# Attention with a learned bias and an expert layer: the expert part of the first two blocks in two halves of d_ff, weights decoded with a Prelu, no arithmetic on GpSimd, a new order

## The chip, the cores and the metric

One core of a Trainium2 chip runs the whole program. The metric is the device time of one execution in microseconds (us), the median of several runs. Engines are named as in the profile: PE (TensorE), DVE (VectorE), ACT (ScalarE), POOL (GpSimd) and SP (SyncE, which here only issues transfers).

## The reference

Attention over 4 batches, 8 heads, 576 positions and 64 dimensions, with a bias that a small network of 32 hidden units makes from the logarithm of the distance of two positions; its output, 2304 tokens of 512, goes through an expert layer with 2048 hidden units.

```python
scores = scale * np.matmul(q, k.transpose(0, 1, 3, 2))
x = (np.log1p(np.abs(rel)) / np.log1p(np.maximum(pos[:, None], 1.0)))[..., None]
bias = np.maximum(x @ w1 + b1, 0.0) @ w2              # 576 x 576 x 8 heads
attn = softmax(scores + bias.transpose(2, 0, 1))       # max subtracted, sum + 1e-9
x = (attn @ v) as 2304 tokens x 512
h = x @ w_in                                           # 512 x 2048, float64 weights
out = (h - np.tanh(h)) @ w_out                         # 2048 x 512, float64 weights
```

## The kernel before

**Precision.** Every large product is taken from fp16 or bf16 halves: a value is split into a high part and the rest (low part), and three products are summed. High parts are written by a scaled copy (`narrow`, L384 on ACT, L385 on POOL, L387 on DVE), low parts by a subtraction (`minus`, L402 POOL, L403 DVE).

**Bias.** 36 groups of 16 positions: four relu instructions of 128 x 576 per group (`hg`, L448 ACT, L450 DVE), 16 matmuls (`pb`, L460), one eviction (`bo`, L469 ACT, L470 DVE) and a store to DRAM (`bias_d`). They are read back by attention as `bt`.

**Weights.** w_in comes as 16 chunks (`wi`: k by c, 512 hidden units each), w_out as 16 (`wo`: f, 128 hidden units each), 512 KB each, as pairs of 32-bit words of a float64. `weight_chunk` makes fp16 halves of one on chip: a shift of the low word (L489, DVE), the sign put into it (L494, DVE), a multiplication of the high word by 2^-111 (L384 to L387), a bit-wise merge of the two (L502, DVE), the high part and the low part. `ws_wi` and `ws_wo` are its staging tiles.

**Attention.** A tile is 128 queries of two heads: scores (`ps`, L588), addition of the bias with the row's extreme (`s`, `mx`, L602, DVE), exp (L616, ACT), reciprocal (L623 and L624), the normalised product as high part (`hl`, L384, ACT) and low part (L632, DVE), a transpose by DMA (`pt`, L642, issued by SP), values (`px`, L664), and the block's input `xt` as high part (L394, ACT) and low part (L682, DVE). k and v are prepared by `prep_kv` (high L384 or L385, low L529, copies and memsets on POOL L536 to L538), q by `prep_q`.

**Expert part.** Tokens come in ten blocks: block 0 has 128 tokens (the half tile t = 4 of the first two batches), blocks 1 to 8 have 256 each, block 9 again 128. `moe(i)` runs over d_ff in groups of 512 columns (four f of block 0, two f of the others): hidden matmuls (`ph`, L703, 24 of 256 tokens or 48 of 128), tanh (`tt`, L715, ACT), h − tanh h (L720, DVE), `gh` (ACT) and `gl` (low part), and output matmuls into one accumulator (`po`, L730), of which there is one buffer. At the end of a block `po` is evicted in two halves (`ot`, L394 and L395) and stored.

**Order.** Nothing above is in program order. A planner (`Plan`) takes each operation with its costs (`c_dve`, `c_act`, ...), the engines that may do it (`WAYS`) and a priority, and lays the operations out by list scheduling; the numbers in `ADJ` are added to the priorities. Each engine then runs its list in order. Tiles share buffers by group (`big`, `row`); `BUFS` says how many there are.

Of the kernel before, what the change touches and what calls it, by code (L numbers as in the profile page):

```python
# [19 lines left out]
P = 128  # L20
# [16 lines left out]
HALF = 4  # L37
# [3 lines left out]
BUFS = {'row': 8, 'big': 12, 'stage': 5, 'hg': 4, 'bt': 3, 'hl': 3, 'pt': 4, 'kv': 8, 'qq': 2, 'mx': 6, 'xt': 6, 'tt': 2, 'gh': 3, 'gl': 3, 'ot': 2}  # L41
# [20 lines left out]
class Op:  # L62
    __slots__ = ("alts", "eng", "cost", "fn", "prio", "deps", "outs", "bufs", "start", "end", "left", "idx", "ready", "port")
# [5 lines left out]
class Plan:  # L69
    LAT = {"pe": 190.0, "dve": 200.0, "act": 60.0, "pool": 60.0, "dma": 0.0}  # L70
# [52 lines left out]
    def op(self, eng, cost=None, fn=None, r=(), w=(), prio=0.0, psum=False):  # L123
# [5 lines left out]
        o.port = {e for e, c, _ in alts if e == "pool" and not isinstance(c, tuple) or e == "dve" and not psum}  # L129
# [29 lines left out]
    def order(self):  # L159
# [6 lines left out]
        hw = xfer = port = 0.0  # L166
# [10 lines left out]
        while done < len(self.ops):  # L177
            moved = False
            claims = {} if loose else self.claimed(cand, now, slots, limit)
            for e in free:  # L180
# [3 lines left out]
                for o in cand[e]:  # L184
                    if o.ready > now or port > now and e in o.port:
                        continue
                    if best is not None and (o.prio, o.idx) >= (best.prio, best.idx):
                        continue
                    if len(o.alts) > 1:
                        mine = now + self.load(e, o.alts[e][0])  # L190
                        if any(
                            max(free[x], now, port if x in o.port else 0.0) + self.load(x, a[0]) < mine
                            for x, a in o.alts.items()
                            if x != e
                        ):
                            continue
# [23 lines left out]
                if isinstance(o.cost, tuple):  # L220
                    issue, move, after, hold = o.cost
                    if e == "dma":
                        hw = max(hw, now) + issue
                        begin = max(hw + 650.0, xfer)
                    else:
                        begin = max(now + SWDGE_HOLD + 650.0, xfer)
                    xfer = begin + move
                    free[e] = now + SWDGE_HOLD if e == "pool" else max(hw, begin + 200.0) if hold else hw
                    o.end = xfer + after
                else:  # L230
                    free[e] = now + o.cost
                    o.end = free[e]
                    if e in o.port:
                        port = o.end
# [13 lines left out]
            if o is not None:  # L248
# [4 lines left out]
                for d in o.outs:  # L253
                    d.left -= 1
                    same = o.eng in d.alts and len(d.alts) == 1 and not isinstance(o.cost, tuple)
                    d.ready = max(d.ready, now + (0.0 if same else lat))
# [45 lines left out]
def kernel(  # L302
# [51 lines left out]
    new_hg = shaped("hg", lambda v: v.rearrange("p (a s) -> p a s", a=2), True)  # L354
    new_bt = shaped("bt", lambda v: v.rearrange("p (a s) -> p a s", a=2))
# [25 lines left out]
    def narrow(n, out, in_, scale=1.0, ptr=0, kind="moe"):  # L381
# [3 lines left out]
            "pool": ("pool", c_pool(n, ptr), lambda: G.tensor_scalar(  # L385
                out(), in_(), scale() if ptr else scale, 1.0, ALU.mult, ALU.mult)),
# [19 lines left out]
    def move(nbytes, out, in_, r=(), w=(), prio=0.0, part=P, hold=(), soft=False):  # L406
# [10 lines left out]
        c = c_dma(nbytes, part)  # L417
# [16 lines left out]
    def bias_group(t, prio):  # L434
# [5 lines left out]
        for j in range(4):  # L440
# [10 lines left out]
                    ("pool", 2400.0,  # L451
                     lambda to=to, src=src, bs=bs: G.tensor_scalar(to(), src, bs, 0.0, ALU.add, ALU.max)),
# [4 lines left out]
        def mms():  # L457
# [7 lines left out]
        op("pe", 1000, mms, r=[(h, y) for h in hgs for y in range(2)] + ["w2"], w=[pb], prio=prio)  # L465
# [6 lines left out]
            r=[pb, "rl"], w=[bo], prio=prio, psum=True,  # L472
        )
        dst = bias_d[16 * t : 16 * t + 16].rearrange("i h k -> (i h) k")
        move(P * S * 4, dst, bo, r=[bo], w=[("bias", t)], prio=prio)


    def weight_chunk(src, hi, lo, key, prio):
# [3 lines left out]
        def words(i, dt=F32):  # L482
# [39 lines left out]
    def prep_kv(b, p, prio):  # L522
# [17 lines left out]
        op("pool", 900.0, split, r=[kw], w=[(kw, 0), (kw, 1)], prio=prio)  # L540
# [27 lines left out]
    def attn_tile(g, t, p, bb, qq, bt, prio):  # L568
# [28 lines left out]
        op("pe", c_mm(HS, 1, 2 * len(terms)) + 190.0, scores, r=rd, w=pss + [(x, "x") for x in rows + [m]], prio=prio)  # L597
        for j in range(2):
# [14 lines left out]
            op("dve", c_psum(S) + 80, bias_min, r=[ps, (bt, 0), (bt, 1)], w=[s, (m, j)], prio=prio - DRAIN, psum=True)  # L613
# [6 lines left out]
            op("act", c_act(S, 1) + 190, expo, r=[(m, j)], w=[s, (m, 2 + j)], prio=prio - 2 * DRAIN)  # L620
# [262 lines left out]
```

## Time and profile before

| | us |
|---|---|
| median of three runs | 682.8 |
| the three runs | 680.49, 682.8, 682.97 |
| span of the profiled execution | 679.7 |
| PE busy | 609.4 |
| DVE busy | 485.8 |
| ACT busy | 422.9 |
| POOL busy | 72.2 |

The profiled execution is one run; its span goes from its first to its last instruction. Busy time of an engine counts its instructions, not its waits. Two neighbouring instructions of DVE or ACT overlap by up to 0.1 us, so that the mean duration of a group is a little above the step from one instruction to the next, which the chain of waits shows.

### The profile page before, as it was taken

Reading aid. Unit: us, or ns where it says so; the run is one execution under the profiler, and the core shown is the slowest. Engines: PE = TensorE matmul, PEld = TensorE weight load, DVE = VectorE, ACT = ScalarE, POOL = GpSimd, SP = SyncE. Lnnn points to the kernel's source line nnn. Section 1 sums busy time; section 2 is a strip of 40 time slices with the busy share of each in tenths; the row PEclk is TensorE's granted clock in tenths of the full one; section 3 lists DMA queues with packets and bytes.
Section 4 is the critical chain, followed back from the end, with each engine's and each line's share of the span. In section 5 each row is a group of like instructions: output and inputs, shape, how many; then the busy total and the mean of one; then the engine's idle time right before and its main releaser. Section 6 shows DMA issues by size and latency. Waiting matters only on the chain.

```text
span 679.7 us, 18908 instructions
## 1 busy us (share of the span) xinstructions
PE 609.4 (90%) x8096; PEld 481.8 (71%) x8096; DVE 485.8 (71%) x1001; ACT 422.9 (62%) x778; POOL 72.2 (11%) x98
## 2 busy tenths in 40 slices
PE   1782546986999999999999999999999999999997
PEld 0221224764787778788888888888888888888897
DVE  4999999799877867677777987677687576433231
ACT  4996667588776667566665767565587575432231
POOL 4400022010100100000111502000010000000000
PEclk9887677998999999999999999999999999999999
DMA  8898886886755887599968799777578379240010
GB/s 315 291 327 304 222 235 109 275 220 140 264 101 121 155 241 115 135 238 196 240 151 219 164 199 180 165 182 156 90 150 213 71 144 209 41 92 2 1 33 17
DMA packets 193779, 114.24 MB, mean 168 GB/s; under 512 B 171152, under 2 KB 176416, under 8 KB 193696
## 3 DMA queue, kind: packets, MB, share of 16 engines
q1 hardware_dynamic: 193632, 113.03, 68.4%
q8 instruction: 63, 1.03, 0.6%
q14 instruction: 20, 0.16, 0.1%
q0 software_dynamic: 64, 0.02, 0.1%
HBM read 55.22 MB, written 15.34 MB: 104 GB/s over the span
## 4 chain that ended last, share of the span: by engine, by line
PE 77%; DVE 15%; DMA 4%; ACT 2%; issue 2%; SPq 0%; ACTq 0%; DVEq 0%
PE ph L703 28%; PE po L730 28%; PE ps L588 11%; PE px L664 8%; PE pb L460 3%; DVE hl L632 2%; DVE s L602 2%; DMA bt<-bias_d 2%; DMA kvst<-kv 1%; DVE hg L450 1%; DVE ws_wo L494 1%; DVE ws_wo L502 1%; DVE bo L470 1%; DVE ws_wi L502 1%; DMA ws_wi<-w_in 1%
## 5 line engine op out<-in xcount | busy, mean ns | idle before, releaser
L703 PE MATMUL ph<-xt,win_hi 128*128 128x256 f16 (+1 forms) x1280 | 193.8, 262 | 2.7 <-DVE xt L682 1.6
L730 PE MATMUL po<-gh,wout_l 128*128 128x256 bf16 (+1 forms) x640 | 162.3, 263 | 1.0 <-DVE wout_l L403 1.0
L730 PE MATMUL po<-gh,wout_h 128*128 128x256 bf16 (+1 forms) x640 | 162.7, 263 | 0.0
L730 PE MATMUL po<-gl,wout_h 128*128 128x256 f16 (+1 forms) x640 | 162.3, 263 | 0.1
L703 PE MATMUL ph<-xt,win_lo 128*128 128x256 f16 (+1 forms) x640 | 161.4, 262 | 0.4 <-DVE win_lo L403 0.4
L616 ACT ACTIVATE s<-s,mx 128x576 f32<-128x576 f32 x144 | 110.7, 769 | 70.2 <-DVE mx L602 69.6
L703 PEld LDWEIGHTS <-win_hi 128*128 128x128 f16 x1280 | 116.6, 98 | 22.3 <-issue 11.3
L730 PEld LDWEIGHTS <-wout_h 128*128 128x128 f16 x1280 | 117.9, 98 | 19.6 <-issue 8.2
L632 DVE SCALAR_TENSOR_TENSOR hl<-s,mx,hl 128x576 f16<-128x576 f32 x144 | 118.3, 854 | 9.4 <-ACT hl L384 9.2
L588 PE MATMUL ps<-kv,qq 64*128 64x288 f16 (+1 forms) x1280 | 91.8, 304 | 27.9 <-DVE mx L602 15.3
L602 DVE CUSTOM_DVE_ANT_0 s<-ps,bt 128x576 f32<-128x576 f32 x144 | 105.0, 752 | 16.4 <-PE ps L588 15.1
L384 ACT ACTIVATE hl<-s,mx 128x576 f16<-128x576 f32 x144 | 104.3, 764 | 8.1 <-issue 3.1
L720 DVE SCALAR_TENSOR_TENSOR tt<-tt,ph 128x512 f32<-128x512 f32 x72 | 49.4, 687 | 80.1 <-ACT tt L715 80.0
L715 ACT ACTIVATE tt<-ph 128x512 f32<-128x512 f32 x72 | 42.9, 596 | 89.4 <-PE ph L703 89.0
L460 PE MATMUL pb<-hg,w2s 128*32 128x288 f32 x576 | 68.1, 453 | 33.7 <-ACT hg L448 23.2
L588 PEld LDWEIGHTS <-qq 64*128 64x128 f16 (+1 forms) x1280 | 56.0, 103 | 55.5 <-issue 27.6
L460 PEld LDWEIGHTS pb<-hg,w2s 128*32 128x32 f32 x576 | 23.2, 114 | 70.9 <-ACT hg L448 44.5
L664 PEld LDWEIGHTS <-kv 128*64 128x64 f16 x2400 | 63.5, 112 | 10.2 <-issue 10.0
L664 PE MATMUL px<-pt,kv 128*64 128x128 f16 (+1 forms) x2400 | 69.0, 217 | 0.6 <-DMA pt<-hl 0.6
L703 PEld LDWEIGHTS <-win_lo 128*128 128x128 f16 x640 | 62.6, 98 | 8.1 <-issue 1.8
L730 PEld LDWEIGHTS <-wout_l 128*128 128x128 f16 x640 | 63.0, 98 | 7.2 <-DVE wout_l L403 1.2
L448 ACT ACTIVATE hg<-zt,b1l 128x576 f32<-128x576 f32 x83 | 59.5, 763 | 0.5 <-DVE win_lo L403 0.5
(54 smaller groups left out, 477.5 us busy)
## 6 DMA issues: line engine op xcount, KB each, us to landing
bt<-bias_d SPq DMA_DIRECT2D x32, 576.0 KB, 4.9
bias_d<-bo SPq DMA_DIRECT2D x36, 288.0 KB, 4.0
kvst<-kv SPq DMA_DIRECT2D x16, 576.0 KB, 7.3
ws_wi<-w_in SPq DMA_DIRECT2D x16, 512.0 KB, 6.4
ws_wo<-w_out SPq DMA_DIRECT2D x16, 512.0 KB, 6.4
bt<-bias_d SPq DMA_DIRECT2D x16, 288.0 KB, 6.1
qst<-qF SPq DMA_DIRECT2D x8, 512.0 KB, 4.3
outT<-ot SPq DMA_DIRECT2D x16, 256.0 KB, 4.7
```

What stands on the lines that cost most here:

```text
L384: "act": ("act", c_act(n, ptr), lambda: A.activation(out(), in_(), AF.Copy, scale=scale() if ptr else scale)),
L448: lambda to=to, src=src, bs=bs: A.activation(to(), src, AF.Relu, bias=bs, scale=1.0)),
L460: nc.tensor.matmul(pb()[32 * j : 32 * j + 32, x, :HS], w2s, hgs[j // 2]()[:, j % 2, x * HS : x * HS + HS], start=True, stop=True, tile_pos ...
L588: nc.tensor.matmul(pss[j]()[w * e : w * e + w, x, :HS], qq()[dp, a, c0 + w * e : c0 + w * e + w], ks()[dp, y, x * HS : x * HS + HS], start ...
L602: V.tensor_tensor_reduce(s().rearrange("p (x k) -> p x k", x=2), ps()[:, :, :HS], bt()[:, j].rearrange("p (x k) -> p x k", x=2), -0.125 / ...
L616: A.activation(s(), s(), AF.Exp, bias=m()[:, j : j + 1], scale=-1.0, accum_out=m()[:, 2 + j : 3 + j])
L632: V.scalar_tensor_tensor(hl()[:, 1, hs], s(), m()[:, 6 + j : 7 + j], hl()[:, 0, hs], ALU.mult, ALU.subtract)
L664: nc.tensor.matmul(px()[64 * j : 64 * j + 64, w * bb : w * bb + w], kw()[:, y, v : v + 64], pt()[:, NCH * l + c, col : col + w], start=(n ...
L703: nc.tensor.matmul(ph()[:, n * (f - f0) : n * (f - f0) + n], w[:, k, f * P : f * P + P], xs[k]()[:, a, :n], start=(k == 0 and e == 0), sto ...
L715: "act", c_actp(512), lambda ph=ph, tt=tt: A.activation(tt(), ph(), AF.Tanh, scale=1.0 / SH),
L720: lambda ph=ph, tt=tt: V.scalar_tensor_tensor(tt(), tt(), -SH, ph(), ALU.mult, ALU.add),
L730: nc.tensor.matmul(po()[:, d // 2, n * (d % 2) : n * (d % 2) + n], wout[w][:, f, d * P : d * P + P], x()[:, n * (f - f0) : n * (f - f0) + ...
```

## The change

- **Two halves.** Blocks 0 and 1 do their first eight f, then their other eight: the expert parts run in the order block 0 first half, block 1 first half, block 0 second half, block 1 second half, block 2 and so on. The accumulator of a first half is evicted into a tile `sum` (two buffers out of the group `big`) and added back when the second half is evicted (L747, DVE). Block 0's first half needs eight chunks of w_in and eight of w_out in place of sixteen each.
- **Prelu.** The sign of a float64's high word and its scaling are done by one ACT instruction: Prelu with scale 2^-111 and alpha 2^32 (L486). The merge then takes the high word shifted by three. It replaces the sign merge on DVE and the multiplication.
- **GpSimd** no longer does relus, scaled copies or subtractions; it keeps the copies and memsets of k and v. High parts of k, v, q and weights may go to ACT or DVE, all subtractions go to DVE.
- **Buffers.** `xt` has eight buffers and the half tiles four of their own (`xh`); `ot` uses tiles of the group `row`.
- **Order.** Costs, latencies and all priorities of the planner are new, and it no longer models a port shared by DVE and POOL.

```diff
+SPLIT = {0: (0, 8, 16), 1: (0, 8, 16)}
+ORDER = [(0, 0), (1, 0), (0, 1), (1, 1)] + [(i, 0) for i in range(2, 10)]
...
 def weight_chunk(src, hi, lo, key, prio):
...
         op(
-            "dve", c_dve2(512),
-            lambda: V.scalar_tensor_tensor(
-                words(0, U32), words(1, U32), 0x80000000, words(0, U32), ALU.bitwise_and, ALU.bitwise_or
-            ),
-            r=[(st, 1)], w=[(st, 0)], prio=prio,
+            "act", c_act(512) + 40.0,
+            lambda: A.activation(words(1), words(1), AF.Prelu, scale=2.0 ** -111, alpha=2.0 ** 32),
+            w=[(st, 1)], prio=prio,
         )
-        op(narrow(512, lambda: words(1), lambda: words(1), 2.0 ** -111, kind="w"), w=[(st, 1)], prio=prio)
...
     def minus(n, out, a, b):
-        return [
-            ("pool", c_pool2(n), lambda: G.tensor_tensor(out(), a(), b(), ALU.subtract)),
-            ("dve", c_dve2(n), lambda: V.tensor_tensor(out(), a(), b(), ALU.subtract)),
-        ]
+        return [("dve", c_dve2(n), lambda: V.tensor_tensor(out(), a(), b(), ALU.subtract))]
...
-    def moe(i, n, col, xs, prio):
+    def moe(i, part, n, col, xs, prio):
...
-        po = new_po(f"po{i}")
-        for f0 in range(0, NF, m):
+        prio += adj(f"m{i}{part}")
+        lo, hi = SPLIT.get(i, (0, NF))[part : part + 2]
+        po = new_po(f"po{i}_{part}")
+        for f0 in range(lo, hi, m):
...
+            if hi < NF and not lo:
+                op(from_psum(2 * n, part_of, src, 1.0 / SO, "out"), r=[po], w=[(acc, h)], prio=top)
+                continue
...
+            if lo:
+                op(
+                    "dve", c_psum(2 * n),
+                    lambda out=out, src=src, part_of=part_of: V.scalar_tensor_tensor(
+                        out(), src(), 1.0 / SO, part_of(), ALU.mult, ALU.add
+                    ),
...
-    "kv": ("act", "pool"),
-    "w": ("act", "pool", "dve"),
-    "q": ("act", "pool"),
+    "kv": ("act", "dve"),
+    "w": ("act", "dve"),
+    "q": ("act", "dve"),
...
-ADJ = {"wo60": -2.382, "wo00": 1.592, "wo130": 0.423, ...
+ADJ = {"b0": 0.6, "b1": -1.081, "b10": 0.173, ...
```

DVE where the first chunks are decoded, before: a chunk's rows are the shift (L489), the sign (L494), the multiplication (L387 onto `ws`), the merge (L502), the high part (L387 onto `wout_h` or `win_hi`) and the low part (L403); the digits behind `wo` or `wi` are the chunk.

```order
L489 TENSOR_SCALAR ws_wo0_0_185<-ws_wo0_0_185 128x512
L502 SCALAR_TENSOR_TENSOR ws_wi3_0_167<-ws_wi3_0_167 128x512
L494 SCALAR_TENSOR_TENSOR ws_wo0_0_185<-ws_wo0_0_185 128x512
L387 TENSOR_SCALAR win_hi_71<-ws_wi3_0_167 128x512
L387 TENSOR_SCALAR ws_wo0_0_185<-ws_wo0_0_185 128x512
L403 TENSOR_TENSOR win_lo_72<-ws_wi3_0_167,win_hi_71 128x512
L502 SCALAR_TENSOR_TENSOR ws_wo0_0_185<-ws_wo0_0_185 128x512
L489 TENSOR_SCALAR ws_wi0_1_238<-ws_wi0_1_238 128x512
L387 TENSOR_SCALAR wout_h_78<-ws_wo0_0_185 128x512
```

The same place after: shift (L481), merge (L491), high part (L384) and low part (L398), with relus (L444) between.

```order
L481 TENSOR_SCALAR ws_wo1_0_236<-ws_wo1_0_236 128x512
L444 TENSOR_SCALAR hg12_323<-zt_80,b1l_76 128x576 x2
L491 SCALAR_TENSOR_TENSOR ws_wo1_0_236<-ws_wo1_0_236 128x512
L444 TENSOR_SCALAR hg14_337<-zt_80,b1l_76 128x576
L384 TENSOR_SCALAR wout_h_78<-ws_wo1_0_236 128x512
L481 TENSOR_SCALAR ws_wo2_0_243<-ws_wo2_0_243 128x512
L398 TENSOR_TENSOR wout_l_79<-ws_wo1_0_236,wout_h_78 128x512
L491 SCALAR_TENSOR_TENSOR ws_wo2_0_243<-ws_wo2_0_243 128x512
```

Chunk wo0 had five DVE rows beside its low part and wo1 now has three; the Prelu of wo1 stands on ACT, among its relus and evictions.

DVE where block 1's input is finished, before: `xt0_0_3` is the last of its four input tiles, and the chunk ahead of it is the last one, wo15.

```order
L489 TENSOR_SCALAR ws_wo15_0_1853<-ws_wo15_0_1853 128x512
L494 SCALAR_TENSOR_TENSOR ws_wo15_0_1853<-ws_wo15_0_1853 128x512
L403 TENSOR_TENSOR wout_l_79<-ws_wo14_0_1757,wout_h_78 128x512
...
L502 SCALAR_TENSOR_TENSOR ws_wo15_0_1853<-ws_wo15_0_1853 128x512
L450 TENSOR_SCALAR hg84_2250<-zt_80,b1l_76 128x576
L682 SCALAR_TENSOR_TENSOR xt0_0_3_2237<-px1_3_2145,xt0_0_3_2237 128x256
L470 TENSOR_SCALAR bo20_2256<-pb20_2239,rls_77 128x576
```

The same place after.

```order
L462 TENSOR_SCALAR bo27_1975<-pb27_1897,rls_77 128x576
L444 TENSOR_SCALAR hg90_1979<-zt_80,b1l_76 128x576
L671 SCALAR_TENSOR_TENSOR xt0_0_3_1994<-px1_3_1909,xt0_0_3_1994 128x256
L384 TENSOR_SCALAR qq0_2_1874<-qst0_2_1875 128x1024
L398 TENSOR_TENSOR qq0_2_1874<-qst0_2_1875,qq0_2_1874 128x1024
L481 TENSOR_SCALAR ws_wo15_0_1880<-ws_wo15_0_1880 128x512
L491 SCALAR_TENSOR_TENSOR ws_wo15_0_1880<-ws_wo15_0_1880 128x512
L384 TENSOR_SCALAR wout_h_78<-ws_wo15_0_1880 128x512
L398 TENSOR_TENSOR wout_l_79<-ws_wo15_0_1880,wout_h_78 128x512
```

All 32 chunks stood ahead of `xt0_0_3` before; now 22 do, and the other ten (wo15, wi12, wi13, wo11, wi23, wi33, wo13, wo12, wo14, wo10) follow it. The instruction is DVE's row 307 before and its row 240 after.

PE at the end of block 1's fourth group of hidden matmuls, before: its output matmuls follow.

```order
L703 MATMUL ph1_6_2598<-xt0_0_3_2237,win_hi_71 128x256
L703 LDWEIGHTS win_lo_72
L703 MATMUL ph1_6_2598<-xt0_0_3_2237,win_lo_72 128x256
L730 LDWEIGHTS wout_h_78
L730 MATMUL po1_2450<-gh1_4_2571,wout_h_78 128x256
```

The same place after: `ph0_8` is the third group (f = 8 to 11) of block 0.

```order
L696 MATMUL ph1_6_2223<-xt0_0_3_1994,win_hi_71 128x256
L696 LDWEIGHTS win_lo_72
L696 MATMUL ph1_6_2223<-xt0_0_3_1994,win_lo_72 128x256
L696 LDWEIGHTS win_hi_71
L696 MATMUL ph0_8_2261<-xt0_4_0_798,win_hi_71 128x128
```

Block 0's second half stands between block 1's first and second.

## Rows read from the trace of the kernel before

**Rows 1.** The page's busy tenths in 40 slices of the span, PE and DVE.

```profile
PE   1782546986999999999999999999999999999997
DVE  4999999799877867677777987677687576433231
```

**Rows 2.** Stretches: us, each engine's busy us, clock, DMA share, GB/s.

```profile
0.00:15.00 15.00, 1.29 (x3) 0.30 (x4) 5.54 (x6) 5.64 (x6) 6.22 (x13) 1.00 0.82 302
15.00:120.20 105.20, 62.21 (x664) 27.56 (x665) 100.92 (x200) 79.79 (x132) 19.20 (x28) 0.77 0.83 248
120.20:176.90 56.70, 47.59 (x807) 35.90 (x807) 50.77 (x108) 42.26 (x75) 6.89 (x8) 0.97 0.79 217
0.00:176.90 176.90, 111.09 (x1473) 63.77 (x1474) 157.22 (x311) 127.69 (x212) 32.31 (x49) 0.86 0.82 243
176.90:250.00 73.10, 73.10 (x965) 56.59 (x965) 55.48 (x117) 51.18 (x94) 6.15 (x6) 1.00 0.74 172
250.00:600.00 350.00, 350.00 (x4503) 292.14 (x4501) 250.71 (x539) 224.25 (x438) 33.74 (x44) 1.00 0.75 162
```

The engines stand in the order PE, weight loads (PEld), DVE, ACT, POOL, with the count of instructions behind each.

**Rows 3.** Chain of waits: start us, us on the chain, what.

```profile
66.13 1.13 DVE qq L403
...
117.58 2.45 DVE hl L632 x2
...
144.21 0.68 DVE tt L720
...
158.47 0.67 DVE s L602
...
163.78 1.46 DVE hl L632 x2
...
165.84 0.43 DVE hg L450
...
168.10 0.37 DVE ws_wo L489
...
169.06 0.60 DVE ws_wo L494
169.66 1.45 DVE bo L470 x2
...
176.87 2.73 PE ph L703 x24
179.59 1.11 PE pb L460 x16
180.70 2.79 PE po L730 x48
```

**Rows 4.** DVE's timeline: start us, us, instruction.

```profile
176.48 0.43 DVE L682 SCALAR_TENSOR_TENSOR xt<-px,xt 128x256 f16<-128x256 f32 x1
```

**Rows 5.** Line 632 over the whole span: shortest, median and longest, ns.

```profile
L632 DVE SCALAR_TENSOR_TENSOR hl<-s,mx,hl x144: 797/814/1714, 77.7 to 601.9; 128x576 f16<-128x576 f32 x144
```

**Rows 6.** Groups to 176.9: busy us, mean ns, idle before and releasers.

```profile
L632 DVE SCALAR_TENSOR_TENSOR hl<-s,mx,hl 128x576 f16<-128x576 f32 x24 | 21.0, 913 | 0.0
L387 DVE TENSOR_SCALAR ws_wi<-ws_wi 128x512 f32<-128x512 f32 x5 | 2.3, 451 | 0.0
...
L448 ACT ACTIVATE hg<-zt,b1l 128x576 f32<-128x576 f32 x68 | 48.6, 762 | 0.5 <-DVE win_lo L403 0.5
L384 ACT ACTIVATE kv<-kvst 128x1152 f16<-128x1152 f32 x7 | 8.1, 1152 | 8.6 <-DMA kvst<-kv 8.6
L384 ACT ACTIVATE ws_wi<-ws_wi 128x512 f32<-128x512 f32 x10 | 6.8, 679 | 2.4 <-issue 1.7 <-DVE ws_wi L494 0.6
...
L402 POOL TENSOR_TENSOR wout_l<-ws_wo,wout_h 128x512 f16<-128x512 f32 x3 | 4.0, 1321 | 15.6 <-DVE wout_h L387 15.4
...
L460 PE MATMUL pb<-hg,w2s 128*32 128x288 f32 x400 | 55.6, 472 | 33.7 <-ACT hg L448 23.2 <-DVE mx L602 6.1 <-DVE hg L450 1.8
```

**Rows 7.** The page's DMA issues: count, KB each, us to landing.

```profile
ws_wo<-w_out SPq DMA_DIRECT2D x16, 512.0 KB, 6.4
```

More of the change, by code (lines that the diff above doesn't have):

```diff
@@ L62 @@
 class Op:
-    __slots__ = ("alts", "eng", "cost", "fn", "prio", "deps", "outs", "bufs", "start", "end", "left", "idx", "ready", "port")
+    __slots__ = ("alts", "eng", "cost", "fn", "prio", "deps", "outs", "bufs", "start", "end", "left", "idx", "ready")
 SWDGE_HOLD = 1040.0
 class Plan:
-    LAT = {"pe": 190.0, "dve": 200.0, "act": 60.0, "pool": 60.0, "dma": 0.0}
+    LAT = {"pe": 200.0, "dve": 118.0, "act": 132.0, "pool": 85.0, "dma": 0.0}
     def __init__(self):
@@ L121, in claimed, with op @@
         return claims
-    def op(self, eng, cost=None, fn=None, r=(), w=(), prio=0.0, psum=False):
+    def op(self, eng, cost=None, fn=None, r=(), w=(), prio=0.0):
         o = Op()
         alts = eng if isinstance(eng, list) else [(eng, cost, fn)]
-        o.port = {e for e, c, _ in alts if e == "pool" and not isinstance(c, tuple) or e == "dve" and not psum}
         o.alts = {e: (c, f) for e, c, f in alts}
@@ L184, in order @@
                 for o in cand[e]:
-                    if o.ready > now or port > now and e in o.port:
+                    if o.ready > now:
                         continue
@@ L191, in order @@
                         if any(
-                            max(free[x], now, port if x in o.port else 0.0) + self.load(x, a[0]) < mine
+                            max(free[x], now) + self.load(x, a[0]) < mine
                             for x, a in o.alts.items()
@@ L220, in order @@
                 if isinstance(o.cost, tuple):
[L221 to L226, printed above, removed]
+                    issue, lead, move, after, hold = o.cost
+                    begin = max(now + (lead if e == "dma" else SWDGE_HOLD + 650.0), xfer)
                     xfer = begin + move
-                    free[e] = now + SWDGE_HOLD if e == "pool" else max(hw, begin + 200.0) if hold else hw
+                    free[e] = now + (SWDGE_HOLD if e == "pool" else issue)
+                    if hold:
+                        free[e] = max(free[e], begin + 600.0)
                     o.end = xfer + after
@@ L255, in order @@
                     same = o.eng in d.alts and len(d.alts) == 1 and not isinstance(o.cost, tuple)
-                    d.ready = max(d.ready, now + (0.0 if same else lat))
+                    d.ready = max(d.ready, now + (SAME[o.eng] if same else lat))
                     if not d.left:
@@ L361 @@
     new_xt = maker("xt", [P, 2, NB], F16)
+    new_xh = maker("xh", [P, 2, P], F16)
     new_tt = maker("tt", [P, 512], F32)
@@ L399, in minus, with move @@
     def minus(n, out, a, b):
[L401 to L406 removed]
+        return [("dve", c_dve2(n), lambda: V.tensor_tensor(out(), a(), b(), ALU.subtract))]
+    def move(nbytes, out, in_, r=(), w=(), prio=0.0, part=P, hold=(), soft=False, store=False):
         def by(q):
@@ L463, in mms @@
                     )
-        op("pe", 1000, mms, r=[(h, y) for h in hgs for y in range(2)] + ["w2"], w=[pb], prio=prio)
+        op("pe", 1110, mms, r=[(h, y) for h in hgs for y in range(2)] + ["w2"], w=[pb], prio=prio)
         src, out = lambda: pb()[:, :, :HS], lambda: bo().rearrange("p (x k) -> p x k", x=2)
@@ L740, in moe @@
+        if hi < NF and not lo:
+            sums[i] = new_sum(f"sum{i}")
+        acc = sums.get(i)
         for h in range(2):
-            ot = new_ot(f"ot{i}_{h}")
-            op(
-                from_psum(2 * n, lambda ot=ot: ot()[:, : 2 * n], lambda h=h: po()[:, h, : 2 * n], 1.0 / SO, "out"),
-                r=[po], w=[ot], prio=top, psum=True,
-            )
+            part_of = lambda h=h: acc()[:, 2 * n * h : 2 * n * h + 2 * n]
+            src = lambda h=h: po()[:, h, : 2 * n]
+            if hi < NF and not lo:
+                op(from_psum(2 * n, part_of, src, 1.0 / SO, "out"), r=[po], w=[(acc, h)], prio=top)
+                continue
+            ot = new_ot(f"ot{i}_{h}") if hi == NF else None
+            out = part_of if ot is None else lambda ot=ot: ot()[:, : 2 * n]
+            if lo:
[4 more added lines that the diff above has]
+                    ),
+                    r=[po, (acc, h)], w=[ot or (acc, h)], prio=top,
+                )
+            else:
+                op(from_psum(2 * n, out, src, 1.0 / SO, "out"), r=[po], w=[ot], prio=top)
+            if ot is None:
+                continue
@@ L753 @@
         bias_group(t, 4.0 + t - BIAS_LEAD)
-    step, col = 0.0, 0
+    step, col, blocks = 0.0, 0, []
     for i, (g, t) in enumerate(BLOCKS):
@@ L776 @@
                     wout_chunk(4 * c + f, WO_P[0] + WO_P[1] * (4 * c + f))
-        moe(i, n, col, xs, 1000.0 + i)
+        blocks.append((n, col, xs))
         col += n
+    for o, (i, part) in enumerate(ORDER):
+        moe(i, part, *blocks[i], 1000.0 + o)
     kernel.plan = plan
```

78 lines of the change are left out of this document (37 added, 41 removed).

## The prediction

> **What bounds the kernel now.** I read the busy slices first. TensorE (PE) is under 90% busy in nine of the first ten of 40 slices and full from then on (but for the last), while VectorE (DVE) is at nine tenths or more in eight of those nine and at seven in the one in which PE is full [rows 1]. The stretches put a time on that turn: block 1, the first full block of the expert part, starts at 176.9. Behind it PE is busy for 73.10 of 73.10 us and then for 350.00 of 350.00; ahead of it PE has 111.09 us of work in 176.90 [rows 2]. So the kernel is two kernels. Behind 176.9 it is worth what PE's work is worth, and no saving on another engine counts. Ahead of it PE lacks 66 us, and the question is who makes it wait. DVE is busy for 157.22 of 176.90 us, ScalarE (ACT) for 127.69; in 15 to 120.2 DVE idles 4.3 us of 105.2 (4.1%), in 120.2 to 176.9 5.9 of 56.7 (10.5%) [rows 2]. The chain of waits agrees: to 174 us it runs mostly through decoding steps on DVE (shift 0.37, sign merge 0.60), relu, evictions and softmax steps, with short hops to ACT and PE, and then through PE alone [rows 3]. The last thing that block 1 waits for is xt0_0_3's low part at 176.48 on DVE [rows 4]. What DVE has to do ahead of that instruction sets the start of block 1.
>
> **The part ahead of block 1.** All counts come from the two orders, up to the DVE instruction that writes xt0_0_3's low part: row 307 before, 240 after. DVE's rows there change as follows, each by its step on the chain [rows 3]:
> - Bit-wise merges 64 to 22, that is 42 × 0.60 = −25.2. Here lies the change: 32 chunks had two each, now 22 chunks have one (Prelu does the sign; ten of w_out's and w_in's chunks come later).
> - The multiplies and shifts of the decoding 43 to 22: 21 × 0.37 = −7.8. High parts 14 to 7: −2.6. Low parts 25 to 22: −1.8.
> - Relus 34 to 45: +4.7. Bias evictions 8 to 6, at 1.45 for two: −1.5.
> - Five high parts of k, v and q that were on ACT or GpSimd: no row has them on DVE; bounds 0.43 (a relu of 576 elements) and 0.86 (twice that, for 1024 or 1152). I take 0.7, nearer to the size: +3.5, range 2.2 to 4.3.
> - Tanh combinations 4 to 2 and low parts 3 to 2 (two groups of block 0 wait for its second half), one eviction into the partial sum: −1.4, by 0.68 and 0.60.
>
> That is −32.1; 157.2 becomes 125.1. Of it Prelu alone is 22 × 0.60 = 13.2, the ten postponed chunks nearly all the rest.
>
> GpSimd loses its arithmetic. One pair of DVE's softmax products took 2.45 us at 117.58, another of the same shape 1.46 at 163.78 [rows 3]; over the kernel the longest single one is 1714 ns against a median of 814 [rows 5]. GpSimd's subtractions are 1.3 us long each [rows 6], and its whole busy time in this part is 32.3 us [rows 2], part of it the copies that stay. How much of DVE's time is such stretching I can only bound: nothing, or 4.8 us (the 24 products here, at a mean of 913, less the median, come to 2.4 [rows 5, 6]; twice that with the other forms). I take 3: DVE has 122.0 us ahead of xt0_0_3.
>
> Now the idle time. In the first 15 us DVE waits for transfers and does 5.5 us, which the change doesn't touch. The other 116.5 us I put at the looser of the two measured shares, 10.5% idle, since with less of its own work DVE waits more often for ACT and PE: 15 + 116.5/0.895 = **145.2 us**, 31.7 earlier than now. At 4.1% idle it would be 136.5, at 15% 152.
>
> ACT: relus 67 to 55 at 0.762, −9.1; k and v high parts 7 to 5 at 1.152, −2.3; evictions 15 to 18 at about the relu's time, +2.2; decoding 30 to 37 at 0.679, +4.8 [rows 6]; a tanh, gh or q less on balance four times, −2.7. Sum −7.1: 127.7 becomes 120.6. No row shows a Prelu; a multiply of its shape on ACT takes 0.679, a relu of 576 elements 0.762 [rows 6], so I take the multiply's and bound it by 0.6 and 0.8: 22 of them move the sum by 2.7 us at most. A Prelu needs only its chunk's load, not the shift, and what is queued behind one that waits for its load are ACT's relus, for which PE's bias matmuls wait, and on DVE the merge of the same chunk. ACT then has 24.6 us idle ahead of block 1 where it has 49.2 now.
>
> **Behind the start of block 1.** From 176.9 to the end of the span are 502.8 us, and PE sets them. Block 0 keeps its second half for later: two groups of hidden and one of output matmuls less than now have been done at the start (3 × 2.79 [rows 3]), +8.4. The split itself adds no matmul. It adds two evictions into partial sums and four additions out of PSUM; the nearest rows are the evictions and a tanh combination of 0.68 [rows 3]. DVE is busy for 251 of 350 us there [rows 2], so I cost them at nothing; without that cover each handing over of the one output accumulator costs up to 0.8 us, two more of them 1.6. Relus and evictions moved between DVE and ACT behind 176.9 are hidden in the same way. So 511.2 us are left from block 1's start.
>
> **What is late next.** Ten chunks now come between block 1's start and its second half, the last of them wo10 (DVE row 307 after, needed by block 0's second half at f = 8 to 11). DVE has until then ten shifts, merges and low parts (15.7), five high parts (1.9), q (1.8, with its measured 1.13), six tanh combinations (4.1), six low parts (3.6), eight relus (3.4), four bias additions (2.8), two softmax products (1.5), 0.9 more: 35.7 us [rows 3], or 36.7 with small waits. PE has ahead of the same point nine groups of block 1 at 2.67, two of block 0 at 2.79 and three groups each of bias and score matmuls at 1.1: 24.0 + 5.6 + 6.6 = 36.2. They are nearly level. At 10.5% idle DVE needs 41.0, and PE stalls for 4.8. I take a **stall of 5**, range 0 to 12: DVE waits less often there than that if PE, which feeds it, never stops.
>
> **Sum.** 145.2 + 511.2 + 5 = 661.4 us of span, against 679.7. The three timed runs lie 0.8 to 3.3 us above the profiled span, with the median 3.1 above: 664.5, rounded to **665 us**, −2.6%.
>
> **Rivals.**
> - *B, ACT takes over.* For it: ACT's 49.2 us of idle time are not spare if they are waits for data that come in lockstep, and 23.2 of PE's 33.7 us of waiting ahead of the bias matmuls end with a relu of ACT's [rows 6]. Against it: ACT has less to do than before, not more, and DVE is the engine that hardly idles. If ACT kept half of its idle time, block 1 would start at 120.6 + 24.6 = 145 as forecast; if it kept 35 to 40 us, at 155 to 160, which gives 675 to 680. If it kept all 49.2, block 1 would start at 169.8 and the time would be 169.8 + 511.2 + 5 + 3.1 = 689: **slower than before**, because the 8.4 us put off and the stall would not be paid for. It decides from a start of 163.5, that is 43 us idle on ACT. A multiply of 512 elements takes 451 ns on DVE and 679 on ACT [rows 6], so the same work moved costs 1.5 times as much there. The Trainium skill (ScalarE: Activation LUTs, Rules for kernel authors) speaks against such a move: it tells to keep relu and multiplications on VectorE, which it gives as up to three times faster for each element in bf16; here, in float32, the rows show 1.5 times, and by that rule this rival would be the outcome.
> - *C, transfers are late.* Ahead of block 1 the DMA moves 176.9 us × 243 GB/s = 43.0 MB [rows 2]; ten chunks of 0.524 MB less [rows 7] are 37.8, which by 145.2 us takes 260 GB/s, more than the 248 of the densest long stretch, less than the 302 of the first 15 us. At 248 block 1 would start at 152 and the time be 672. Between block 1's start and wo10 SyncE's queue carries ten chunks, seven bias stores and one q, 7.8 MB: 36 us at 217 GB/s, as in 120.2 to 176.9, but 48 at the 162 of the steady part [rows 2]: a stall of 12 and not 5, with the rest as forecast 672. Both in part: 672 to 676.
> - *D, DVE stays as dense as in 15 to 120.2* (4.1% idle): start 136.5, 656; without the stall 651. For it: the waits in 120.2 to 176.9 come from PE's and ACT's steps of the last tiles, which are fewer per us of DVE's work after a cut of the decoding only if the order is a good one.
> - *E, the gain is given back*: the order of another fit makes PE wait somewhere behind 250 us, where now it never does. That takes 15 us or more of new waits, against 72% of DVE's time and 64% of ACT's in use there: 680 to 686.
>
> **How the numbers follow.** Forecast (656 to 672) 0.58; C beyond it (672 to 676) 0.10; B in part (675 to 680) 0.12; B in full (about 689) 0.08; D (651 to 656) 0.07; E (680 to 686) 0.05. Range 652 to 681: it leaves out B in full, most of E and a little of D, 0.15. A measurement of this kernel tells about 0.5% from no change, so faster is under 679.4 and slower over 686.2: faster 0.58 + 0.10 + 0.12 + 0.07 less 0.02 of B at the bound = 0.85; slower 0.08; the same 0.07.
>
> **What would show it.** Right: xt0_0_3's low part at 140 to 152 us; DVE busy for 119 to 125 us ahead of it, ACT for 118 to 124; PE full from there but for one or two waits of 0 to 12 us in all, ahead of block 0's second half, that end with a low part of w_out; no softmax product on DVE at twice its median. Prelu between 0.6 and 0.8 us. Wrong: ACT over 90% busy in 15 to 145, or the chain of waits running through ACT's relus and Prelus (B); DVE and ACT both idle ahead of shifts that a DMA ends (C); PE idle behind 250 us (E). If the start of block 1 comes at 145 but the time is 675 or more, the mistake lies in what I cost at nothing behind it.

## The result and the profile after

The changed kernel takes **657.3 us** in the median (four runs, 655.6 to 659.7), the kernel before 682.2 in the same comparison: a ratio of 0.9642, 95% interval 0.9617 to 0.9668. That is 3.6% faster; 665 was forecast, with a range of 652 to 681. The profiled execution has a span of 653.9 us, 25.8 less than before.

The page's busy slices, PE, DVE and ACT, answer to [rows 1]:

```profile
PE   1666578889999999999999999999999999999997
DVE  4999999969988677888989787878785564223231
ACT  4999789969778677686877676677774553222221
```

PE is full from the tenth of 40 slices on (one of them is now 16.3 us). The stretches answer to [rows 2], with block 1 starting at 142.25; columns as there:

```profile
0.00:15.00 15.00, 1.56 (x3) 0.36 (x4) 6.65 (x7) 6.00 (x7) 4.02 (x15) 1.00 0.83 304
15.00:142.25 127.25, 91.96 (x1327) 53.50 (x1326) 114.99 (x245) 112.03 (x196) 7.47 (x17) 0.84 0.95 258
0.00:142.25 142.25, 93.52 (x1329) 53.87 (x1330) 121.65 (x251) 118.03 (x202) 11.48 (x31) 0.86 0.94 263
142.25:215.35 73.10, 73.10 (x964) 59.55 (x964) 67.12 (x143) 60.66 (x111) 0.00 (x0) 1.00 0.73 204
215.35:574.00 358.65, 358.65 (x4927) 297.52 (x4926) 263.16 (x575) 232.30 (x453) 7.38 (x24) 1.00 0.83 169
574.00:653.90 79.90, 75.93 (x882) 70.00 (x880) 21.11 (x31) 18.76 (x31) 0.00 (x0) 0.99 0.06 18
...
126.00:142.25 16.25, 13.42 (x233) 7.43 (x234) 11.44 (x24) 12.69 (x20) 0.00 (x0) 1.00 1.01 247
142.25:180.00 37.75, 37.75 (x433) 31.28 (x433) 36.74 (x76) 32.26 (x57) 0.00 (x0) 1.00 0.71 247
```

Ahead of block 1 DVE works 121.65 us where it worked 157.22, ACT 118.03 for 127.69. Behind its start PE never stops until the last few matmuls; 511.65 us pass there, against 502.8 before. DVE's timeline at the two points on which the sum rested (the first answers to [rows 4]), and the chain of waits there:

```profile
141.60 0.42 DVE L671 SCALAR_TENSOR_TENSOR xt<-px,xt 128x256 f16<-128x256 f32 x1 [0.97 <-ACT xt L391]
...
176.97 0.69 DVE L398 TENSOR_TENSOR wout_l<-ws_wo,wout_h 128x512 f16<-128x512 f32 x1
```

```profile
127.72 0.67 ACT hg L442
...
128.44 1.16 PE pb L452 x10
...
139.35 1.80 PE px L653 x60
141.15 1.11 PE pb L452 x16
142.25 5.35 PE ph L696 x48
...
178.73 2.79 PE po L723 x48
```

The input of block 1 is complete at 142.0. The second row is the low part of wo10, done at 177.7, for which block 0's second half asks at 178.7: PE came 1.0 us behind it and did not wait.

The last 16 us ahead of block 1 are not DVE's. The chain leaves DVE at 125.9 us, runs through ACT to the end of a relu at 128.4, and from there mostly through PE; in 126 to 142.25 DVE is busy for 11.44 of 16.25 us, and the transfers are full. When the input is complete, PE still has 0.2 us of bias matmuls ahead of block 1.

### The profile page after: what moved, and what is told of

Same layout as the page of the kernel before. It is cut to its first block, busy times and chain, and to the rows that moved or that the text cites. A ratio compares the mean times of both kernels' runs of the same rounds, so it can differ in the third digit from the quotient of the medians.

```text
span 653.9 us, 18849 instructions
## 1 busy us (share of the span) xinstructions
PE 601.2 (92%) x8096; PEld 480.9 (74%) x8096; DVE 473.0 (72%) x998; ACT 429.7 (66%) x796; POOL 18.9 (3%) x55
## 4 chain that ended last, share of the span: by engine, by line
PE 83%; DVE 9%; ACT 4%; issue 1%; DMA 1%; SPq 0%; ACTq 0%; DVEq 0%
PE ph L696 29%; PE po L723 28%; PE ps L577 12%; PE px L653 9%; PE pb L452 5%; DVE hl L621 2%; DVE s L591 2%; ACT hg L442 1%; DMA kvst<-kv 1%; DVE hg L444 1%; ACT hl L383 1%; DVE ws_wi L491 1%; DVE ws_wo L491 1%; ACT s L605 1%; DVE bo L462 1%
## 5 line engine op out<-in xcount | busy, mean ns | idle before, releaser
L723 PEld LDWEIGHTS <-wout_h 128*128 128x128 f16 x1280 | 116.1, 98 | 21.1 <-issue 9.9
L621 DVE SCALAR_TENSOR_TENSOR hl<-s,mx,hl 128x576 f16<-128x576 f32 x144 | 113.3, 813 | 13.8 <-ACT hl L383 13.8
L452 PE MATMUL pb<-hg,w2s 128*32 128x288 f32 x576 | 62.6, 460 | 41.3 <-ACT hg L442 29.2
L577 PE MATMUL ps<-kv,qq 64*128 64x288 f16 (+1 forms) x1280 | 89.9, 301 | 6.6 <-DVE mx L591 2.9
L383 ACT ACTIVATE gh<-tt 128x512 bf16<-128x512 f32 x72 | 45.0, 625 | 26.1 <-DVE tt L713 25.9
```

The source lines that it names most:

```text
L383: "act": ("act", c_act(n, ptr), lambda: A.activation(out(), in_(), AF.Copy, scale=scale() if ptr else scale)),
L452: nc.tensor.matmul(pb()[32 * j : 32 * j + 32, x, :HS], w2s, hgs[j // 2]()[:, j % 2, x * HS : x * HS + HS], start=True, stop=True, tile_pos ...
L577: nc.tensor.matmul(pss[j]()[w * e : w * e + w, x, :HS], qq()[dp, a, c0 + w * e : c0 + w * e + w], ks()[dp, y, x * HS : x * HS + HS], start ...
L621: V.scalar_tensor_tensor(hl()[:, 1, hs], s(), m()[:, 6 + j : 7 + j], hl()[:, 0, hs], ALU.mult, ALU.subtract)
L723: nc.tensor.matmul(po()[:, d // 2, n * (d % 2) : n * (d % 2) + n], wout[w][:, f, d * P : d * P + P], x()[:, n * (f - f0) : n * (f - f0) + ...
```

## The experiments

Two theories stood against each other: that DVE's instructions ahead of block 1 set its start, so that the time follows DVE's work there, and that what sets it is something that DVE shares with others (ACT, the transfers, the order in which all of them wait for each other). In the table, the start of block 1 is the moment at which its input is complete (the end of `xt0_0_3`'s low part on DVE), and the busy times are those ahead of it; PE idle is what lies between that moment and the end of the span. PE begins block 1's hidden matmuls within 1 us of it, but for three kernels in which work of block 0 comes between: a_nosplit (164.3), a_neither (177.0) and b_prelu (185.0).

| kernel | median us | ratio to before (95%) | start | DVE | ACT | PE idle behind |
|---|---|---|---|---|---|---|
| before | 682.2 | 1 | 176.9 | 157.2 | 127.7 | 4.5 |
| after | 657.3 | 0.9642 (0.9617 to 0.9668) | 142.0 | 121.4 | 118.0 | 3.9 |
| a_nosplit | 678.4 | 0.9942 (0.9915 to 0.9969) | 142.5 | 121.8 | 115.5 | 15.2 |
| a_noprelu | 682.2 | 1.0001 (0.9988 to 1.0014) | 168.1 | 143.8 | 127.3 | 5.2 |
| a_neither | 696.2 | 1.0200 (1.0167 to 1.0233) | 172.0 | 147.7 | 129.0 | 11.7 |
| a_oldadj | 681.0 | 0.9972 (0.9953 to 0.9992) | 167.0 | 137.8 | 125.7 | 4.3 |
| b_prelu | 686.7 | 1.0071 (1.0046 to 1.0096) | 182.2 | 153.3 | 124.8 | 7.3 |
| b_nosign | 673.9 | 0.9876 (0.9858 to 0.9894) | 169.6 | 139.6 | 126.3 | 4.3 |
| b_prelu16 | 677.4 | 0.9931 (0.9914 to 0.9948) | 172.8 | 148.6 | 126.5 | 4.3 |
| x_dve | 674.6 | 0.9888 (0.9859 to 0.9918) | 156.3 | 136.3 | 118.9 | 7.1 |
| x_act | 672.8 | 0.9866 (0.9845 to 0.9888) | 153.9 | 123.1 | 131.6 | 6.2 |
| x_pool | 667.8 | 0.9792 (0.9763 to 0.9820) | 155.4 | 135.8 | 118.6 | 4.0 |
| x_dma | 666.8 | 0.9781 (0.9755 to 0.9806) | 153.0 | 121.5 | 118.1 | 4.0 |
| a_sixpool | 655.5 | 0.9602 (0.9577 to 0.9627) | 142.9 | 119.4 | 118.1 | 3.9 |

Kernels whose name begins with a are the kernel after with an edit, b the kernel before with one; x are the kernel after with work added in the same order of every engine.

### Taking the parts out

**a_nosplit**

```diff
-SPLIT = {0: (0, 8, 16), 1: (0, 8, 16)}
-ORDER = [(0, 0), (1, 0), (0, 1), (1, 1)] + [(i, 0) for i in range(2, 10)]
+SPLIT = {}
+ORDER = [(i, 0) for i in range(10)]
```

> The kernel after with the split taken out: ten blocks in their order, each with all of d_ff at once; Prelu, the engines of every operation and all other priorities as after. Theory 'DVE sets the start of block 1, PE the rest': the ten chunks come back ahead of block 1, which is 10 x (0.37 + 0.60 + 0.60) plus some five high parts of 0.37 on DVE, 17.6 us more; at the 90% density of DVE that the kernel after shows ahead of block 1 the start moves from 142.3 to about 162, PE has 8.4 us less left behind it: about 668 us. Rival 'the new priorities are what helps, the split nothing': 655 to 660. Rival 'the priorities fit only the split order': 675 or more, with PE idle behind the start of block 1.

Measured 678.4: 10 us over the first theory's 668, and what its second rival says (675 or more, with PE idle behind the start). Block 1's input is ready at the same time as with the split, with 22 chunks ahead of it in both. But block 0 must now go through all of d_ff first, and its hidden matmuls wait for further chunks: PE comes to block 1 at 164.3, with 29 chunks and 140.7 us of DVE's work done by then. That is near the first theory's 162; but what PE waits for are weights, not block 1's input, and more is lost behind 164.3, in waits and at a lower clock, than the theory has. From the moment at which the input is ready (columns as in [rows 2]):

```profile
142.50:186.20 43.70, 32.52 (x353) 22.67 (x346) 37.13 (x80) 34.91 (x59) 0.00 (x0) 0.80 0.65 235
```

```profile
PE ph L696 <- DVE win_hi L384: 5.7, 2, 4.1
PE ph L696 <- DVE win_lo L398: 1.8, 3, 0.8
```

The second fence lists the two largest of PE's waits behind it (us, times, longest). In 43.7 us PE works 32.5; of the 11.2 that it idles, 7.5 are hidden matmuls that wait for high and low parts of w_in. With these waits the granted clock is 0.80 there, a mean over the levels 2.4 and 1.2 GHz, and PE's busy time over the span is 608.3 us where it is 601.2 after, for the same matmuls. So the split is worth 21 us here: 11.2 of waits, 7.1 of PE's longer work, which goes with the lower clock, and 2.8 of PE's work that had not been done when the input was ready.

**a_noprelu** puts the sign merge (DVE) and the multiplication (ACT or DVE) back in place of the Prelu.

> The kernel after with the decoding of before: the sign merge back on DVE and the multiplication on ACT or DVE as the planner chooses; the split and all priorities as after. Theory 'DVE sets the start': 22 chunks x 0.60 = 13.2 us more on DVE ahead of block 1, at 90% density 14.6 us, and up to 8 us more if the multiplications go to DVE; ten more merges behind it, 6 us, of which some becomes a stall ahead of the second halves: 672 to 680 us. Rival 'ACT sets it' (ACT is relieved of some multiplications, so nothing is lost): 655 to 662.

Measured 682.2, a little above the first theory's range. The whole loss is the start, 26.1 us later, with 22.4 us more of DVE's work ahead of it: the sign merges, multiplications, and 26 chunks in place of 22. Behind the start little changes (1.3 us more of PE's idle time).

**a_neither** is both edits together.

> The kernel after with both taken out, the split and the Prelu; no arithmetic on GpSimd and the new priorities stay. Theory 'DVE sets the start', with parts that add up: 657 + 11 (split) + 21 (32 sign merges of 0.60 at 90% density) = 689 us, more if multiplications go to DVE. Rival 'the new order is what gained': 660 to 670. Rival 'ACT or PE form a floor, the parts do not add': 675 to 682.

Measured 696.2, more than the first theory's 689. With the Prelu, the split is worth 21.1 us, without it 14.0; the Prelu 24.9 with the split and 17.8 without. They don't add up: 38.9 for both, 46 for the two one by one. What is left of the change without the two parts (the order, the buffers, GpSimd's arithmetic moved to DVE and ACT) is 14 us slower than the kernel before, so the rest, fitted to the whole, brings nothing by itself; which of it costs the 14 us is not shown.

**a_oldadj** has the table ADJ of before in the kernel after.

> The kernel after with the priorities (the table ADJ) of before; split, Prelu, engines and costs of the planner as after. Theory 'the split and the Prelu bring the gain, the fit of the priorities less than half of it': block 1 starts 5 to 10 us later than in the kernel after, 662 to 670 us. Rival 'without priorities fitted for it the new code gains nothing' (as the Prelu alone under the priorities of before, 686.7): 678 to 690.

Measured 681.0: the first theory's 662 to 670 is wrong, and the rival right. With the priorities of before, 29 chunks and not 22 are decoded ahead of block 1 (137.8 us of DVE), although the split would let them wait; and PE waits more often. Its waits in 15 to 167, and after's in 15 to 142.25:

```profile
PE pb L452 <- ACT hg L442: 17.3, 14, 2.8
PE pb L452 <- DVE mx L591: 11.5, 5, 7.2
PE px L653 <- DMA pt<-hl: 8.5, 2, 6.1
PE ps L577 <- ACT bo L461: 7.1, 6, 3.1
```

```profile
PE pb L452 <- ACT hg L442: 15.9, 8, 5.8
PE pb L452 <- ACT bo L461: 5.5, 4, 2.6
PE ps L577 <- DVE mx L591: 2.9, 6, 0.9
PE ps L577 <- ACT bo L461: 2.8, 3, 1.5
```

So the split and the Prelu make the gain possible, and the priorities collect it. The other way round holds too: **b_prelu**, the Prelu alone in the kernel before, under priorities fitted without it.

> The kernel before with the Prelu alone (in place of the sign merge and the multiplication); GpSimd, the order of the blocks, costs and priorities as before. DVE loses 32 x 0.60 and some 11 multiplications of 0.37 ahead of block 1, 23 us; ACT gains 16 x 0.67 = 10.7, from 127.7 to 138.4. Theory 'DVE sets the start' alone: 26 us earlier, 656 us. Rival 'ACT takes over as soon as DVE is relieved': ACT is at most about as dense as the 83% that it reaches in the kernel after, so block 1 starts at 167 and the time is about 672. No gain (680 to 684) if the priorities of before fit only their own costs.

Measured 686.7, 0.7% slower than before. DVE is relieved of 32 sign merges, but ahead of block 1 it works 153.3 us and not some 134: in the planner's new order ten more relus (44 for 34) and the first scores of the next tiles stand there, and a load of w_out is issued only at 145.2. DVE's merge of that chunk comes late with it, and behind the merge, in DVE's order, stands the low part of w_in for which block 0's hidden matmuls ask. Its chain of waits there (start us, us, what):

```profile
145.23 7.58 DMA ws_wo<-w_out
...
152.84 0.70 ACT ws_wo L494
...
153.57 0.69 DVE ws_wo L499
154.26 0.61 DVE win_lo L403
...
154.92 4.45 PE ph L700 x40
```

To see the Prelu without a new order, the next two keep the order of before on every engine.

### The same order, with less or more work

**b_nosign** leaves the sign merges out; **b_prelu16** does without them where the multiplication stood on ACT already and could be a Prelu.

```diff
# b_nosign: the planner counts the merge, and nothing is issued
+        plan.ops[-1].alts["dve"] = (c_dve2(512), lambda: None)
```

> The kernel before with the very same order on every engine; the 32 sign merges are left out and nothing is put in their place, so that all weights keep a positive sign. All 32 stand ahead of block 1: DVE has 19.2 us less to do there, no engine has more. Theory 'DVE sets the start of block 1 also before' (10.5% idle): 21.5 us earlier, 661 us. Rival 'lockstep': doubling a step on ACT cost the kernel after nearly as much as on DVE, so that ACT and the transfers give back half: 670 to 673. Rival 'another engine': 679 to 683.

> The kernel before with the very same order on every engine; where the multiplication of a chunk already stood on ACT (16 of 32 chunks) it is a Prelu, and the sign merge of that chunk is gone from DVE. 9.6 us less on DVE, nothing more on ACT. Theory 'DVE sets the start': 10.7 us earlier, 671.5 us. If the 686.7 us of the Prelu alone came from Prelu itself and not from the order that the planner then chose: 682 to 687. Lockstep: 676 to 678.

Measured 673.9 and 677.4, that is 8.7 and 5.1 us less than the kernel before beside them (682.6): 40% and 48% of what DVE alone would give. So the Prelu itself loses nothing where the order stays; b_prelu's loss came with the order that the planner then chose. In b_nosign DVE has 17.6 us less ahead of block 1, and the start comes 7.3 us earlier. DVE's idle time in 15 us to the start grows from 10.2 to 21.0:

```profile
15.00:169.60 154.60, 108.08 (x1470) 63.16 (x1468) 133.60 (x273) 120.25 (x206) 27.12 (x35) 0.83 0.86 248
```

So in the kernel before DVE was not alone in setting the start, although it idled least. The four x kernels ask the same of the kernel after.

```diff
# x_dve: the low part of every chunk is written twice
+        op([(e, cost, lambda: (sub(), sub()))], ...)
# x_act: behind each Prelu
+                     A.activation(words(1), words(1), AF.Copy, scale=1.0)),
# x_pool: for the 22 chunks ahead of block 1, into a place that is written later
+            op("pool", 1300.0, lambda: G.tensor_tensor(wout["l"][:, 10, :], hi(), hi(), ALU.subtract), ...)
# x_dma: for the same chunks
+                G.dma_start(spare[f], w_out[P * (f % NF) : P * (f % NF) + P, :256])
```

> The kernel after with the very same order on every engine; DVE writes the low part of every weight chunk twice (one subtraction of 0.60 more for each of 32 chunks, 22 of them ahead of block 1). Theory 'DVE sets the start of block 1': 13.2 us of DVE more, at its density of 90% the start moves by 14.6; behind it ten more, 6 us on an engine that is 97% busy there, a stall of 5: 672 to 677 us. Rival 'ACT or the transfers set it': DVE takes the 13.2 us out of its own idle time, 657 to 661.

> The kernel after with the very same order on every engine; ACT copies the high words onto themselves behind every Prelu (one ACT instruction of 0.60 to 0.67 more for each of 32 chunks, 22 of them ahead of block 1). Theory 'DVE alone sets the start of block 1': ACT takes the 14 us out of the 24 us that it idles there, 657 to 661 us. Rival 'ACT is as tight as DVE': the start moves by 14 to 16 us, 671 to 677. In lockstep, with either engine waiting for the other in turn, half of it: 663 to 667.

> The kernel after with the very same order on every engine; GpSimd, idle otherwise, does a subtraction of 128 x 512 for each of the 22 chunks ahead of block 1, whose result nobody reads: 22 x 1.3 us. Theory 'arithmetic on GpSimd stretches DVE's instructions beside it': DVE's softmax products ahead of block 1 go from a mean of 811 ns to 900 or more, single ones to 1.2 us or more, DVE has 3 to 6 us more to do and the time is 660 to 664 us. Rival 'the stretching has another cause' (transfers, the order): no product over 830 ns, 656 to 659.

> The kernel after with the very same order on PE, DVE, ACT and SP; GpSimd issues a copy of 256 KB from DRAM to DRAM for each of the 22 chunks ahead of block 1, 5.8 MB on top of 37 MB. Theory 'the transfers are full (DMA 95% busy there) but nobody waits for them': 657 to 662 us. Rival 'the transfers set the start': 15% more to move in 127 us, 19 us later, 672 to 680.

From 15 us to the start of block 1, in the order x_dve, x_act, x_pool, x_dma (each from its own kernel):

```profile
15.00:156.30 141.30, 96.30 (x1326) 53.22 (x1324) 129.74 (x267) 113.04 (x197) 7.58 (x17) 0.79 0.86 238
...
15.00:153.90 138.90, 97.00 (x1326) 54.49 (x1324) 116.64 (x245) 125.79 (x219) 7.66 (x17) 0.78 0.92 236
...
15.00:155.40 140.40, 95.56 (x1325) 53.32 (x1322) 128.64 (x244) 112.19 (x196) 44.68 (x39) 0.79 0.86 237
...
15.00:153.00 138.00, 89.48 (x1326) 51.88 (x1325) 115.08 (x245) 112.39 (x197) 20.49 (x39) 0.86 0.99 280
```

x_dve came as the first theory says (14.9 us more on DVE, start 14.3 later, 3.2 us more of PE's waits behind, 674.6). x_act refutes "DVE alone": 13.6 us more on ACT delay the start by 11.9, although ACT had 24 us idle there. x_dma refutes "nobody waits for the transfers": DMA 99% busy, DVE and ACT with the same work as after, and a start 11.0 us later for 5.8 MB more. Full transfers alone would have cost 19 by the estimate put down for it, so a part of it fell into slack. The waits of DVE and ACT name what they waited for, first in x_act, then in x_dma; in the kernel after none of either kind is longer than 0.8 us from 15 us to the start:

```profile
DVE win_lo L398 <- ACT win_hi L383: 3.7, 6, 0.8
DVE wout_l L398 <- ACT wout_h L383: 2.4, 1, 2.4
```

```profile
DVE bo L464 <- DMA bt<-bias_d: 7.0, 1, 7.0
...
ACT ws_wo L488 <- DMA ws_wo<-w_out: 5.7, 1, 5.7
...
DVE ws_wo L483 <- DMA ws_wo<-w_out: 5.2, 2, 4.5
```

x_pool costs 10.4 us though nobody reads what GpSimd writes: DVE's same instructions take 14.3 us longer (below). Ahead of block 1 DVE, ACT and the transfers are each the limit for some of the time, in an order in which they wait for each other; the 9.6% of DVE's time and 12% of ACT's that are idle in 15 to 142.25 are not spare.

**a_sixpool** takes six low parts that are needed late from DVE to GpSimd, in the order of after.

> The kernel after with the same order; six low parts of chunks that are needed late (three of w_in's third and one of its fourth quarter, wo8 and wo9) are subtracted on GpSimd, which is idle, and not on DVE. DVE loses 6 x 0.60 = 3.6 us ahead of block 1. Theory 'GpSimd's arithmetic costs DVE about 0.38 us for each us that it runs' (22 subtractions, 37.6 us on GpSimd, gave DVE 14.3 us more): 6 x 1.4 to 1.7 us stretch DVE by 3 to 4 us, so nothing is won, 656 to 659 us. Rival 'idle GpSimd time is free': DVE 3.6 us less, 653 to 655.

Measured 655.5 (five runs, 653.8 to 656.4), between the two theories, ratio 0.9602 with an interval that overlaps that of after. DVE ahead of block 1 has 2.0 us less, not 3.6, and the start is no earlier (142.9 for 142.0). It is at least not slower; a gain over the kernel after is not shown.

## Why the prediction was right, point by point

- **What bounds it: right.** Behind block 1's start PE is busy for 73.10 of 73.10 and 358.65 of 358.65 us, and the rest takes 511.65 us where the sum had 511.2. The two evictions into partial sums and four additions cost PE no wait, as put.
- **DVE's work: right.** 122.0 us forecast, 121.65 measured; ACT 120.6 forecast, 118.03 measured. High parts of q took 684 ns and of k and v 784 on DVE (taken at 0.7), the Prelu 654 to 767 ns (taken at 0.68). No softmax product on DVE is longer than 819 ns, where [rows 5] had one of 1714. The rows are the Prelu's line and the products' line over the whole span (shortest, median and longest ns, first and last start):

```profile
L486 ACT ACTIVATE ws_wi<-ws_wi x16: 654/670/767, 22.3 to 154.5; 128x512 f32<-128x512 f32 x16
```

```profile
L621 DVE SCALAR_TENSOR_TENSOR hl<-s,mx,hl x144: 797/812/819, 67.8 to 544.4; 128x576 f16<-128x576 f32 x144
```

- **Idle share: nearly right, in part by luck.** 9.6% in 15 to 142.25, taken at 10.5%. It is the mean of two unlike stretches, which the sum did not tell apart: 6.7% in 15 to 126, and 30% in the last 16 us, where the chain is ACT's and PE's. The start came 3.0 us ahead of the forecast 145.2: 1.3 because DVE did 6.65 us of its work in the first 15 us and not 5.5, 0.4 because it had 0.35 us less to do, 1.2 from the idle share.
- **The stall: the term that was mis-sized.** 5 us forecast, none measured. The step that failed gave DVE the idle share of 120.2 to 176.9, a stretch in which DVE waited for PE, to a stretch in which PE never stops. There DVE is busy for 36.74 of 37.75 us, as dense as it needs to be, and wo10 is in time by 1.0 us. The two sums that were set against each other, 36.7 us of DVE and 36.2 of PE, were good (35.6 and 36.5 us passed). x_dve shows how little DVE has to spare there: with six more us it is busy for 42.7 of the 43.7 us to 200, and PE waits 3.2, though for evictions, relus and score steps that come late with it and for no part of a chunk.
- **The sum.** 664.5 less 657.3 is 7.2: 3.0 from the start, 5.0 from the stall, less 0.5 of PE's rest and 0.3 of the distance from span to median (3.4 measured, 3.1 taken).
- **The reason: right in its number, too simple in its cause.** The sum divides DVE's work by a density and thereby takes ACT and the transfers to follow. In one order they don't: 17.6 us off DVE in the kernel before gave 7.3 (b_nosign). Nor is xt0_0_3's low part alone what PE waited for, since PE's own bias matmuls ahead of block 1 ended 0.2 us later. The forecast held because its counts came from the changed kernel's own order, in which ACT's work and the bytes ahead of block 1 fall as well, and because the density stayed near the measured one. The priorities alone decide between 657 and 681 (a_oldadj); the prediction gave them no term of their own.
- **Rival B** (ACT takes over) did not come: ACT idles 24.2 us ahead of block 1, 24.6 by the sum. Its mechanism is real all the same, as x_act shows. The rule named beside it, in the Trainium skill (ScalarE: Activation LUTs, Rules for kernel authors), to keep multiplications on VectorE, did not decide here: the Prelu takes 0.67 us on ACT, and gives back a merge and a multiplication of 0.69 and 0.45 on DVE.
- **Rival C** (transfers late) did not come either: 263 GB/s ahead of block 1, where 260 were needed. x_dma shows that there was little more to be had.
- **Rivals D and E**: DVE is 9.6% idle and not 4.1%, and no wait of PE stands behind 215 us but those of the tail.

**What stays open.** The priorities were fitted to the whole change. How far a fit of its own would bring a_nosplit or a_noprelu was not tried, so that 21 and 25 us are what the parts are worth in this order and not what each would bring alone. The GpSimd part was not undone by itself; x_pool bounds it from one side.

## What to carry to other kernels

Of an engine that looks like the bound (little idle time, most of the chain), ask what one us less of it gives in the same order: leave a step out, or write one twice on each engine in turn. Where a doubled step costs nearly its full length on each of several engines, the stretch is balanced, and a cut pays in full only together with an order that is fitted to it; a good edit under the old order can even lose. Work that the steady, PE-bound part can hide is best moved there: splitting the reduction of the first blocks lets ten of 32 weight chunks be decoded beside matmuls that run anyway, and keeps PE from waiting, at a lower clock, for each of them.

## What the runs showed of the hardware that was not expected

GpSimd and DVE hold each other up in both directions. In x_pool 22 subtractions take 37.6 us on GpSimd, between 1.04 and 6.75 each, and DVE's work ahead of block 1 grows by 14.3 us. Of DVE's 251 instructions there, 19 take over 0.15 us longer than in the kernel after, none by more than 0.85, and each of the 19 overlaps a subtraction of GpSimd in time. The longest, in GpSimd's timeline, and then DVE's at its end and a little later (both of x_pool):

```profile
80.33 6.75 POOL L500 TENSOR_TENSOR wout_l<-win_hi 128x512 f16<-128x512 f16 x1 [4.11 <-ACT win_hi L384]
87.16 1.37 POOL L500 TENSOR_TENSOR wout_l<-wout_h 128x512 f16<-128x512 f16 x1
```

```profile
85.16 0.68 DVE L492 SCALAR_TENSOR_TENSOR ws_wi<-ws_wi 128x512 uint32<-128x512 uint32 x1
85.76 0.42 DVE L482 TENSOR_SCALAR ws_wo<-ws_wo 128x512 uint32<-128x512 uint32 x1
86.22 1.41 DVE L492 SCALAR_TENSOR_TENSOR ws_wo<-ws_wo 128x512 uint32<-128x512 uint32 x1
...
90.11 1.52 DVE L399 TENSOR_TENSOR wout_l<-ws_wo,wout_h 128x512 f16<-128x512 f32 x1
91.56 1.00 DVE L615 TENSOR_SCALAR mx<-mx 128x2 f32<-128x2 f32 x1
```

While DVE issues back to back, at its usual 0.68 and 0.42, GpSimd's subtraction hangs for 6.75 us; then it is DVE's merge that takes 1.41, a low part 1.52 and an instruction on 2 elements, usually 0.17, a whole us. It hits what DVE happens to run then, not one form: relus reach 1292 ns, while the 24 softmax products, 1714 ns at worst in the kernel before, stay at 811 in the mean. The Trainium skill (GPSIMD Engine Reference, Specifications) says that GpSimd shares its SBUF interfaces with VectorE, with contention when a DVE instruction runs in a two-port mode or has two SBUF inputs; the rows agree for the merges and low parts, which have two. The relus and the instruction on 2 elements read one tile; whether they run in a two-port mode no run here shows.
